# An S4 convolution and a shift mixer in one kernel: two of four inverse groups of the first half moved from the last steps of a loop to behind it

## The chip, the cores and the metric

The kernel runs on one core of a Trainium2 chip. The core has five engines that run side by side, each through its own list of instructions, in order: PE (TensorE, matrix products), DVE (VectorE), ACT (ScalarE), POOL (GpSimd) and SP (SyncE, which here issues most of the DMAs). An instruction that waits for a semaphore holds up everything behind it on its own engine. The metric is the time of one execution on the device in microseconds (us). The kernel before took 711.11 us, the median of three runs between 710.77 and 711.17.

## The reference

One batch of 2048 tokens with 512 channels passes through two blocks, each behind a layer norm that is scaled and shifted by a vector made from a condition `c`, and each added back to the input:

```python
sa, ca, ga, sb, cb, gb = split of silu(c) @ w_mod
h = layernorm(x) * (1 + ca) + sa
x = x + ga * A(h)          # A: convolution over the tokens
h = layernorm(x) * (1 + cb) + sb
x = x + gb * B(h)          # B: token shift mixer, then channel MLP

# A: K[d, l] = Re sum_n C[d, n] * exp(dt*A[d, n]*l) * dt*B[d, n], N = 128
Yf = rfft(pad(u)) * rfft(pad(K));  y = irfft(Yf)[:, :L] + u * Dskip
# B, with D = 512, F = 1376
h = gelu(layernorm(x) @ w1)
g0..g3 = the four quarters of h's channels, shifted by +1, -1, +2, -2 tokens
x1 = x + concat(g0..g3) @ w2
out = x1 + gelu(layernorm(x1) @ w3) @ w4
```

All of it is float32.

## The kernel before

*Matrix products.* The kernel makes its float32 products either directly, or, for the four weights W1 to W4, in three passes: each operand is split into a high part (rounded to the faster type fp32r) and a low part, and high times high, low times high and high times low are summed (`three`, L825, L826, L828). The high part of a split is an ACT copy, the low part a DVE subtraction.

*The convolution* is a Fourier transform cut in stages. First the kernel K and the input are brought into spectra in part; then a loop of 16 steps, `steps = [(jh, kc)]`, goes over two halves of the channels (`jh`, 256 channels each, steps 0 to 7 and 8 to 15) and eight blocks of frequencies (`kc`). A step multiplies the spectrum of K (`spectrum_k`, L667, TensorE) with that of the input (`multiply`, L678, L679 and L683, DVE), takes the previous step's product a stage back (`back`, L693, TensorE, written to a scratch tensor `ZT[jh]` in memory by a POOL DMA), prepares the next step's input spectrum (`spectrum_u`, L644) and loads a block three steps ahead (`load_vu`).

*The inverse groups.* What is left of the inverse transform of a half is done in four groups of four token blocks (there are 16 token blocks of 128 tokens). `load_inv(jh, g)` reloads two blocks of `ZT[jh]`; `inv_half(jh, g, i, ...)` makes eight matmuls (L722) into one PSUM tile and returns a function that, when called, lets DVE add that tile to the resident sequence `X2`, which the trace calls `KX` (L725). `inverse(jh, g)` does both halves `i` of a group, matmuls and addition in turn. The loop makes groups 0, 1 and 2 of the first half in steps 11, 12 and 13, with their loads issued in steps 9 to 12. Group 3 is made behind the loop, and so are all groups of the second half.

*Memory that several stages share.* Loaded blocks lie in a ring of seven buffers (`block`, named `ld`): the VU blocks, the reloaded blocks of `ZT`, and the raw halves of W1 and W2 (`ldw1`, `ldw2` with `two`) on their way to being split. A buffer is used again when its last reader is done. When the convolution is over, the pools that hold the ring are closed (`a2.close()`, `a12.close()`) and the weights W3 and W4 (`pw34`) are laid over their memory; the tile of W4's low part, which is also where W4's raw values are loaded, covers the addresses of the ring.

*The tail.* From the end of the loop on the order is written out by hand. `back` of step 15; the reload of `ZT[1]`; inverse group 3 of the first half; ten `half_stat` (L772), which take the layer norm's statistics over the first 256 channels of one token block each; the second half of W2 is loaded (`split = ldw2(two, 2, 2)`), and its `split()` stands further down; `keep(n)` (L1139), n matmuls whose result is not used; the inverse groups of the second half. Then the mixer runs over eight groups of 256 tokens, in the order 7, 0, 1, 2, 3 here and 4, 5, 6 inside the channel groups: `mix_mod1`, `mix_mod2` (scale and shift, statistics on DVE, the reciprocal root and the negated mean on POOL, L814 and L815), `mix_norm` (ACT), `transposed` (TensorE, L790: eight transposes of a 128x128 tile, each an entry of (channel block k, token block i), into two PSUM tiles, the first for k = 0 and 1, the second for k = 2 and 3), `parts_of` (ACT's copy and DVE's subtraction, L798), `mix_half` (twice 48 matmuls with W1 through `mix_w`, then gelu to a tile `go`, and its store to a scratch tensor `GD` by SP, L837). `load_w(c)` issues a third of W3's and W4's loads on SP (L738). The shift by 1 or 2 tokens is made by reading `GD` at an offset: `chan_load(g)` issues four loads of the windows of a channel group (L860), `chan_split` splits them (the ACT copy `wh`), and `chan_sum` multiplies them with W2 (L879, L880, L882).

*The channel groups.* `chan(0)` to `chan(7)`, 256 tokens each, run W3 (L825, L826, L828) and W4 (L941, L942, L949) with gelu between, and carry along the next group's preparation.

All engines take their work in the order in which the code emits it (`tc.manual_schedule()`): there is no planner, and no due times.

Of the kernel before, what the change touches and what calls it, by code (L numbers as in the profile page):

```python
# [111 lines left out]
def body(ctx, tc, A):  # L112
# [403 lines left out]
    for k in range(8):  # L516
        w, i = ("w3", k) if k < 4 else ("w4", k - 4)
        n = A[w].shape[0] // 4
# [182 lines left out]
    def load_inv(jh, g, i=None, qs=(Y, Y)):  # L701
        if (jh, g) not in zis:
            zis[jh, g] = [block() for h in range(2)]
        for h in range(2):
            c0 = 12 - 4 * g if h == 0 else 4 * g
            a, n = (0, 4) if i is None else (2 * (i if h else 1 - i), 2)
            qs[h].dma_start(zis[jh, g][h][:, a:a + n],
                            dram(ZT[jh], (h * 16 + c0 + a) * 32768, [[256, 128], [32768, n], [1, 256]]))
# [6 lines left out]
    def inv_half(jh, g, i, pl, name):  # L715
        zz = zis[jh, g]
        p = pl.tile([128, 2, 256], F32, name=name)
        for e in range(2):
            for h in range(2):
                b = g * 4 + i * 2 + e  # L720
                cc = 15 - b if h == 0 else b
                T.matmul(p[h * 64:h * 64 + 64, e], FI[:, cc, h], zz[h][:, cc % 4],  # L722
                         start=True, stop=True, skip_group_check=True)
        x = X2[:, g * 4 + i * 2:g * 4 + i * 2 + 2, jh * 256:jh * 256 + 256]
        return lambda: V.tensor_add(x, p, x)  # L725

    def inverse(jh, g):
        for i in range(2):
            inv_half(jh, g, i, psy, "py")()

    def weights(pl, src, rows, cols, name, ntile):
        hi = pl.tile([128, ntile, cols], F32R, name=name + "h")
# [38 lines left out]
    def half_stat(b, jh):  # L771
        V.bn_stats(st1[:, (b + 2) % 16, jh], X2[:, b, jh * 256:jh * 256 + 256])  # L772
# [12 lines left out]

    def transposed(x):
        ps = [psT.tile([128, 2, 256], F32, name=f"pT{j}") for j in range(2)]
        for k in range(4):
            for i in range(2):
                T.transpose(ps[k // 2][:, k % 2, i * 128:i * 128 + 128], x[:, i, k * 128:k * 128 + 128], ident)  # L790
        return ps

# [290 lines left out]
    with tc.manual_schedule():  # L1083
        t3 = A["T3"].rearrange("p (a b) -> p a b", a=32)
        load_vu(*steps[0])
        Y.dma_start(T3[:, :16], t3[:, :16])
        Y.dma_start(Gm, A["G"].rearrange("p (a b) -> p a b", a=2))
        for r in range(8):
            k_first(r)
            if r == 3:  # L1090
                load_vu(*steps[1])
            if r == 6:
                load_vu(*steps[2])
        us = spectrum_u(*steps[0])
        split = None
        for n, st in enumerate(steps):
            p = spectrum_k(*st)
            multiply(*st, us, p)
            if n == 7:
                v0x.close()  # L1100
                pw2 = ctx.enter_context(pool("pw2", side="right", reuse_waits="tile"))
                pw1 = ctx.enter_context(pool("pw1", side="right", reuse_waits="tile"))
                W2h, W2l, ldw2 = weights(pw2, A["w2"], 512, 512, "w2", 4)
                W1h, W1l, ldw1 = weights(pw1, A["w1"], 512, 512, "w1", 4)
            if n > 0:
                back(*steps[n - 1])
            if n < 15:
                us = spectrum_u(*steps[n + 1])
            if n + 3 < 16:
                load_vu(*steps[n + 3])  # L1110
            if n == 0:
                load_t2(1)
            if n == 1:
                Y.dma_start(T3[:, 16:], t3[:, 16:])
            if n in (3, 4, 6, 8):
                load_x(n - 3 if n < 5 else n // 2 - 1)
            if n == 9:
                Y.dma_start(FI, A["FI"].rearrange("p (a b c) -> p a b c", a=16, b=2))
            if split:
                split()  # L1120
                split = None
            if n in (8, 9, 14):
                split = (ldw1 if n < 10 else ldw2)(two, n % 2 * 2, 2)
            if 9 <= n < 13:
                load_inv(0, n - 9)
            if 11 <= n < 14:
                inverse(0, n - 11)
        back(*steps[15])
        s2x.close()
        tp = lambda name, bufs=1, **k: pool(name, bufs, reuse_waits="tile", **k)  # L1130
        cm = ctx.enter_context(tp("cm", 2, side="right"))
        hv = ctx.enter_context(tp("hv", side="right"))
        gop = ctx.enter_context(tp("gop", 2, side="right"))
        psT = ctx.enter_context(tp("psT", space=PSUM))
        psw = ctx.enter_context(tp("psw", 2, space=PSUM))
        def keep(n):
            d = psT.tile([128, 2, 256], F32, name="pT0").rearrange("p a b -> p (a b)")
            for _ in range(n):
                T.matmul(d, W1h[:, 0, :128], W1h[:, 0], start=True, stop=True)  # L1139

        load_inv(1, 3, 1, (Y, S))
        load_inv(1, 0, 0, (Y, S))
        load_inv(1, 3, 0)
        load_inv(1, 0, 1)
        inverse(0, 3)
        for b in (14, 15, 0, 1, 2, 3, 4, 5, 6, 7):
            half_stat(b, 0)
        load_inv(1, 1)
        split = ldw2(two, 2, 2)
        keep(14)  # L1150
        inv_half(1, 3, 1, psy, "py")()
        first_stats(7)
        load_inv(1, 2)
        a00 = inv_half(1, 0, 0, psy, "py")
        a30 = inv_half(1, 3, 0, psw, "pm")
        a01 = inv_half(1, 0, 1, psw, "pm")
        keep(22)
        mix_mod1(7)
        mix_mod2(7, 0)
        mix_mod2(7, 1)  # L1160
        a00()
        mix_norm(7)
        first_stats(0)
        a30()
        a01()
        mix_mod1(0)
        hl = parts_of(transposed(mh.pop(7)[0]))
        mix_mod2(0, 0)
        mix_mod2(0, 1)
        split()  # L1170
        a10 = inv_half(1, 1, 0, psy, "py")
        a11 = inv_half(1, 1, 1, psy, "py")
        mix_half(7, hl, 0)
        mix_norm(0)
        first_stats(1)
        a10()
        mix_half(7, hl, 1)
        mix_mod1(1)
        hl = parts_of(transposed(mh.pop(0)[0]))
        mix_mod2(1, 0)  # L1180
        mix_mod2(1, 1)
        a11()
        mix_half(0, hl, 0)
        a20 = inv_half(1, 2, 0, psy, "py")
        mix_norm(1)
        first_stats(2)
        mix_half(0, hl, 1)
        a21 = inv_half(1, 2, 1, psy, "py")
        mix_mod1(2)
        hl = parts_of(transposed(mh.pop(1)[0]))  # L1190
        mix_mod2(2, 0)
        a20()
        mix_mod2(2, 1)
        a21()
        a2.close()
        a12.close()
        pw34 = ctx.enter_context(tp("pw34"))
        W3h, W3l, ldw3 = weights(pw34, WD["w3"], 512, 1376, "w3", 4)
        W4h, W4l, ldw4 = weights(pw34, WD["w4"], 1376, 512, "w4", 11)
        c2p = ctx.enter_context(tp("c2p", 2))  # L1200
        psm = ctx.enter_context(tp("psm", 2, space=PSUM))
        load_w(0)
        mix_half(1, hl, 0)
        mix_norm(2)
        first_stats(3)
        mix_half(1, hl, 1)
        chan_load(0)
        mix_mod1(3)
        hl = parts_of(transposed(mh.pop(2)[0]))
        mix_mod2(3, 0)  # L1210
        mix_mod2(3, 1)
        load_w(1)
        load_w(2)
        mix_half(2, hl, 0)
        chan_split(0)
        mix_norm(3)
        chan_mod(0, 0)
        mix_half(2, hl, 1)
        add0 = chan_sum(0, 0)
        chan_mod(0, 1)  # L1220
        add0()
        hl = parts_of(transposed(mh.pop(3)[0]))
        add1 = chan_sum(0, 1)
        split_w(1)
        n = cm.tile([128, 2, 512], F32, name="h2")
        sm = [(cm.tile([128, 2], F32, name="cmv"), cm.tile([128, 1], F32, name="crs")) for i in range(2)]

        def stat0(i):
            stats(sm[i][0], cn[0][:, i])
            rstd(sm[i][1], sm[i][0][:, 1:2])  # L1230

        def norm0(i):
            V.tensor_scalar(n[:, i], cn[0][:, i], sm[i][0][:, 0:1], sm[i][1], op0=OP.subtract, op1=OP.mult)

        stat0(0)
        split_w(1)
        add1()
        mix_half(3, hl, 0)
        stat0(1)
        norm0(0)  # L1240
        norm0(1)
        split_w(1)
        mix_half(3, hl, 1)
        r = transposed(n)
        split_w(1)
        r = parts_of(r)
        split_w(4)
        chan_add(0)
        first_stats(4)
        chan_load(1)  # L1250
        for g in range(8):
            r = chan(g, r)
# [18 lines left out]
```

## Time and profile before

| what | us |
|---|---|
| median of three runs | 711.11 |
| the profiled execution | 710.0 |
| its span, first to last instruction | 708.2 |
| TensorE busy | 670.5 (95%) |
| its weight loads | 518.3 (73%) |
| DVE busy | 500.1 (71%) |
| ACT busy | 336.0 (47%) |
| POOL busy | 91.5 (13%) |

A profile shows one execution. "Span" is the time from the first to the last instruction; the execution's own time is a little longer. A matmul's weight load runs beside other matmuls and is listed apart. A row of a timeline gives the start in us, the duration, the engine, the line of the code, the operation with its output and inputs by the program's names, and after x how many instructions of that kind are run together in the row; the bracket at the end says how long the engine had been idle ahead of it and what released it, the releaser being inferred. A row whose engine reads DMA is a transfer, from its issue's completion to its landing. A row whose engine ends in q, as SPq, is the queue of that engine issuing DMAs or waiting to. In a table by stretches each row is one stretch of time, with the busy time of each engine in it and the number of instructions in brackets.

### The profile page before, as it was taken

To read this page: it belongs to the slowest core of one execution; us is meant where nothing else is said; L and a number is where in the kernel's file an instruction comes from. 1 tells how busy PE (TensorE), PEld (TensorE's weight loads), DVE (VectorE), ACT (ScalarE), POOL (GpSimd) and SP (SyncE) were. 2 spreads that over 40 slices of the span, in tenths; PEclk is the share of its full clock that TensorE was granted. 3 is DMA by queue.
4 is the path that set the end of the run, shared out by engine and by line. 5 is a ranking of instruction groups with operands and counts; after the bars stand their busy time and mean duration, and the time that the engine had idled before them with its cause. 6 is when DMAs were issued, how large, how long until landed. Compare 5 with 4: busy or idle time off the path is not lost.

```text
span 708.2 us, 16836 instructions
## 1 busy us (share of the span) xinstructions
PE 670.5 (95%) x7083; PEld 518.3 (73%) x7083; DVE 500.1 (71%) x827; ACT 336.0 (47%) x553; POOL 91.5 (13%) x203
## 2 busy tenths in 40 slices
PE   1899999999999999997999899999999999999997
PEld 0456655666568655654788789899898988989896
DVE  7799999999986765776988868467454536354522
ACT  3878898889956454542444633314132221212120
POOL 4011112021000000000563101001020000000000
PEclk9999999999999999999999999999999999999999
DMA  8903274745349997965559211011110201111011
GB/s 285 285 2 83 65 219 117 199 103 174 84 105 348 252 274 259 300 208 184 189 187 321 65 31 31 16 45 31 39 52 16 60 16 36 25 31 31 0 31 31
DMA packets 56627, 85.51 MB, mean 121 GB/s; under 512 B 5508, under 2 KB 43400, under 8 KB 54888
## 3 DMA queue, kind: packets, MB, share of 16 engines
q1 hardware_dynamic: 52536, 66.87, 33.4%
q0 software_dynamic: 3136, 16.52, 6.7%
q8 instruction: 56, 0.92, 0.6%
q10 hardware_dynamic: 880, 1.05, 0.5%
q14 instruction: 19, 0.16, 0.1%
HBM read 58.20 MB, written 31.85 MB: 127 GB/s over the span
## 4 chain that ended last, share of the span: by engine, by line
PE 46%; DMA 4%; DVE 2%; ACT 1%; SPq 1%; issue 1%; ACTq 0%; DVEq 0%
PE pm L825 7%; PE pm L826 7%; PE pm L828 7%; PE pa L949 6%; PE pa L941 6%; PE pa L942 6%; PE ph L880 2%; PE ph L882 2%; PE ph L879 2%; DMA GD<-go 2%; PE pT L790 2%; DMA ld<-ZT 1%; DMA w4l<-Dw 1%; PE pT L1139 1%; SPq L738 1%
## 5 line engine op out<-in xcount | busy, mean ns | idle before, releaser
L120 ACT ACTIVATE gh<-pm 128x512 fp32r<-128x512 f32 (+1 forms) x48 | 26.9, 561 | 200.6 <-PE pm L828 200.6
L825 PE MATMUL pm<-nh,w3h 128*128 128x256 f32 (+1 forms) x352 | 85.8, 279 | 0.9 <-ACT nh L120 0.9
L826 PE MATMUL pm<-nh,w3l 128*128 128x256 f32 (+1 forms) x352 | 85.7, 279 | 0.1
L933 DVE TENSOR_TENSOR gl<-gf,gh 128x512 fp32r<-128x512 f32 (+1 forms) x48 | 30.8, 642 | 68.4 <-ACT gf L120 68.4
L941 PE MATMUL pa<-w4h,gh 128*128 128x512 f32 (+1 forms) x176 | 69.6, 396 | 0.0
L942 PE MATMUL pa<-w4l,gh 128*128 128x512 f32 (+1 forms) x176 | 68.9, 392 | 0.0
L825 PEld LDWEIGHTS pm<-nh,w3h 128*128 128x128 f32 (+1 forms) x352 | 65.3, 185 | 2.6 <-ACT nh L120 1.1
L826 PEld LDWEIGHTS pm<-nh,w3l 128*128 128x128 f32 (+1 forms) x352 | 65.3, 185 | 2.2 <-DVE w3l L744 0.5
L828 PE MATMUL pm<-nl,w3h 128*128 128x256 f32 (+1 forms) x352 | 54.8, 277 | 0.0
L949 PE MATMUL pa<-w4h,gl 128*128 128x512 f32 (+1 forms) x176 | 48.1, 390 | 0.8 <-DVE gl L933 0.8
L457 PE MATMUL xx<-MG,ON 64*128 64x512 f32 x160 | 48.1, 397 | 0.0
L458 PE MATMUL xx<-MG,ON 64*128 64x512 f32 x160 | 48.0, 396 | 0.0
L753 POOL TENSOR_TENSOR rs<-mv,eps_t 128x1 f32<-128x1 f32 (+1 forms) x39 | 11.9, 306 | 277.8 <-DVE mv L759 265.8
L828 PEld LDWEIGHTS pm<-nl,w3h 128*128 128x128 f32 (+1 forms) x352 | 46.7, 185 | 0.2 <-DVE nl L798 0.2
L885 DVE TENSOR_TENSOR h<-h,ph 128x512 f32<-128x512 f32 x16 | 11.0, 687 | 45.1 <-PE ph L882 45.1
L475 DVE SCALAR_TENSOR_TENSOR e<-tr,p 128x512 f32<-128x512 f32 x64 | 41.0, 682 | 1.5 <-ACT tr L120 1.4
L120 ACT ACTIVATE z<-pz 128x512 f32<-128x512 f32 x32 | 17.4, 595 | 51.9 <-issue 25.1
L678 DVE TENSOR_TENSOR ma<-pk,us 128x512 f32<-128x512 f32 x32 | 21.9, 685 | 27.3 <-issue 16.1
L507 PEld LDWEIGHTS kp<-e,e 128*32 128x32 f32 x2048 | 30.1, 110 | 12.7 <-issue 8.2
L949 PEld LDWEIGHTS pa<-w4h,gl 128*128 128x128 f32 (+1 forms) x176 | 33.0, 188 | 8.3 <-DVE gl L933 1.2
L484 DVE TENSOR_TENSOR e<-tr,p 128x1024 f32<-128x1024 f32 x32 | 38.9, 1216 | 0.0
L485 DVE TENSOR_TENSOR e<-tr,m 128x1024 f32<-128x1024 f32 x32 | 38.9, 1216 | 0.0
(230 smaller groups left out, 1758.3 us busy)
## 6 DMA issues: line engine op xcount, KB each, us to landing
VU<-vs SPq DMA_DIRECT2D x64, 128.0 KB, 3.4
ld<-VU SPq DMA_DIRECT2D x16, 512.0 KB, 14.5
ZT<-z POOLq DMA_DIRECT2D x15, 512.0 KB, 6.3
ld<-ZT SPq DMA_DIRECT2D x12, 512.0 KB, 6.2
Dw<-in_w POOLq DMA_DIRECT2D x8, 688.0 KB, 4.7
xu<-in_u SPq DMA_DIRECT2D x16, 256.0 KB, 8.1
KX<-in_u SPq DMA_DIRECT2D x16, 256.0 KB, 12.6
GD<-go SPq DMA_DIRECT2D x16, 256.0 KB, 2.2
```

The costliest lines, as they stand in the source:

```text
L120: return S.activation(out, in_, f, bias=bias, scale=scale)
L457: T.matmul(x[:, :512], la, ma, start=(i == 0), stop=(i == len(ops) - 1))
L458: T.matmul(x[:, 512:], lb, mb, start=(i == 0), stop=(i == len(ops) - 1))
L475: V.scalar_tensor_tensor(e0[:, 1, a], tr[:, 1, 0], 1.0 - 2.0 * a, mg[:, a], op0=OP.mult, op1=OP.mult)
L484: V.tensor_mul(e0[:, 0], tr[:, 0, 0:1].to_broadcast([128, 2, 512]), mg)
L485: V.tensor_mul(e1.rearrange("p r d q -> p r (d q)"), tr[:, :, 1], m1s[0][:, u % 2:u % 2 + 1].to_broadcast([128, 2, 512]))
L825: T.matmul(p, wh[:, k, c], hi[k], start=(k == 0), stop=False)
L826: T.matmul(p, wl[:, k, c], hi[k], start=False, stop=False)
L828: T.matmul(p, wh[:, k, c], lo[k], start=False, stop=(k == 3))
L941: T.matmul(acc[i], gh[:m, e, s], W4h[:m, f], start=(f == 0), stop=False)
L942: T.matmul(acc[i], gh[:m, e, s], W4l[:m, f], start=False, stop=False)
L949: T.matmul(acc[i], gl[:m, e, s], W4h[:m, f], start=False, stop=(f == 10))
```

## The change

It does five things.

1. Inverse groups 1 and 2 of the first half leave steps 12 and 13. Group 1's 16 matmuls are issued in step 15, behind `back` of step 14, and its two additions behind the loop, ahead of `back` of step 15. Group 2 goes ahead of group 3, behind the loop. Their reloads of `ZT[0]`, and group 3's, move from steps 10, 11 and 12 to steps 13, 13 and 14.
2. Four of the ten `half_stat` (token blocks 0 to 3, which belong to group 0) go into step 12; six stay in the tail.
3. The two fillers get shorter: `keep(14)` becomes `keep(6)`, and `keep(22)` becomes `keep(14)`.
4. The eight transposes of `transposed` are issued by token block, i = 0 with all four k first, then i = 1, where before each k came with both i. It applies to every mixer group and every channel group.
5. The `split()` of W2's second half moves from ahead of the inverse group (1, 1) to behind the last addition of the convolution, `a21()`, just ahead of the closing of the pools.

```diff
+    def inverse_parts(jh, g):
+        return [inv_half(jh, g, i, psy, "py") for i in range(2)]
+
     def inverse(jh, g):
-        for i in range(2):
-            inv_half(jh, g, i, psy, "py")()
+        for f in inverse_parts(jh, g):
+            f()
...
     def transposed(x):
         ps = [psT.tile([128, 2, 256], F32, name=f"pT{j}") for j in range(2)]
-        for k in range(4):
-            for i in range(2):
+        for i in range(2):
+            for k in range(4):
...
             if n > 0:
                 back(*steps[n - 1])
+            if n == 15:
+                i1 = inverse_parts(0, 1)
...
-            if 9 <= n < 13:
-                load_inv(0, n - 9)
-            if 11 <= n < 14:
-                inverse(0, n - 11)
+            if n == 9:
+                load_inv(0, 0)
+            if n == 11:
+                inverse(0, 0)
+            if n == 12:
+                for b in range(4):
+                    half_stat(b, 0)
+            if n == 13:
+                load_inv(0, 1)
+                load_inv(0, 2)
+            if n == 14:
+                load_inv(0, 3)
+        for f in i1:
+            f()
         back(*steps[15])
...
         load_inv(1, 0, 1)
+        inverse(0, 2)
         inverse(0, 3)
-        for b in (14, 15, 0, 1, 2, 3, 4, 5, 6, 7):
+        for b in (14, 15, 4, 5, 6, 7):
             half_stat(b, 0)
         load_inv(1, 1)
         split = ldw2(two, 2, 2)
-        keep(14)
+        keep(6)
         inv_half(1, 3, 1, psy, "py")()
...
-        keep(22)
+        keep(14)
         mix_mod1(7)
...
         mix_mod2(0, 1)
-        split()
         a10 = inv_half(1, 1, 0, psy, "py")
...
         a21()
+        split()
         a2.close()
```

`inverse` now emits the matmuls of both halves ahead of the first addition; the order on TensorE and the order on DVE are each the same by that.

## The prediction

> **What bounds the kernel now.** Three views, in this order: the page's head and chain, the stretches of the steps and of what follows, and the timelines between the last steps and the first channel group.
>
> ```profile
> span 708.2 us, 16836 instructions
> PE 670.5 (95%) x7083; PEld 518.3 (73%) x7083; DVE 500.1 (71%) x827; ACT 336.0 (47%) x553; POOL 91.5 (13%) x203
> PE 46%; DMA 4%; DVE 2%; ACT 1%; SPq 1%; issue 1%; ACTq 0%; DVEq 0%
> ...
> 290.77:298.20 7.43, 7.43 (x106) 4.63 (x104) 6.65 (x14) 4.89 (x14) 0.72 (x2) 1.00 1.04 352
> 298.20:305.63 7.43, 7.43 (x106) 4.63 (x104) 5.21 (x10) 2.80 (x8) 0.53 (x1) 1.00 0.95 289
> 305.63:313.06 7.43, 7.43 (x106) 4.63 (x104) 5.20 (x10) 2.80 (x8) 0.53 (x1) 1.00 0.89 297
> 313.06:318.76 5.70, 5.70 (x90) 3.48 (x88) 4.31 (x9) 1.72 (x5) 0.34 (x1) 1.00 0.07 24
> ...
> 345.01:404.00 58.99, 55.45 (x410) 49.15 (x410) 50.80 (x96) 31.93 (x53) 24.98 (x64) 1.00 0.55 177
> 404.00:708.20 304.20, 298.89 (x1911) 269.33 (x1911) 158.74 (x262) 74.59 (x139) 17.82 (x46) 1.00 0.11 30
> ```
>
> TensorE is the bound. Columns of the stretches: length, then busy time of PE, its weight loads, DVE, ACT and POOL, granted clock, DMA share, GB/s. The first four are steps 11 to 14, cut at the first L667 matmul of each: TensorE is busy for all of a step, and a step with an inverse group is 1.73 us longer (7.43 against 5.70). From 404 us on TensorE works 298.89 of 304.20 us with the other engines well below, so whatever moves the start of that stretch moves the end of the kernel one for one. The change touches only what lies between 298 and 404 us, where TensorE does wait:
>
> ```profile
> 320.67 1.99 PE L693 MATMUL pz<-zc,Gm 64*128 64x512 f32 x8
> 324.48 1.99 PE L693 MATMUL pz<-zc,Gm 64*128 64x512 f32 x8 [1.82 <-ACT w2h L120]
> 326.39 1.95 PE L722 MATMUL py<-ld,FI 128*64 128x256 f32 x16
> 328.27 3.47 PE L1139 MATMUL pT<-w1h 128*128 128x512 f32 x14
> 333.54 3.09 PE L722 MATMUL py<-ld,FI 128*64 128x256 f32 x16 [1.80 <-DMA ld<-ZT]
> 339.57 5.28 PE L1139 MATMUL pT<-w1h 128*128 128x512 f32 x22
> 345.01 1.06 PE L790 MATMUL pT<-ident,h 128*128 128x128 f32 x8
> 346.00 1.95 PE L722 MATMUL py<-ld,FI 128*64 128x256 f32 x16
> 372.10 0.98 PE L790 MATMUL pT<-ident,h 128*128 128x128 f32 x7 [1.08 <-ACT h L120]
> ```
>
> There is a hole of 1.82 us between the last two `back` calls, filler (`keep`, L1139) of 3.47 and 5.28 us around the reload of ZT, and a wait for a normalised tile. The hole's releaser is misnamed: `back(15)` needs DVE's third `zc`, which ends at 324.33 (row below).
>
> **The change, part by part.** I keep the clock of the old trace and subtract the loop's gain at the end.
>
> *The loop.* Steps 12 and 13 lose an inverse group each: 2 x (7.43 - 5.70) = 3.46 us. Does another engine take over? Step 12 gets four half statistics, at 0.337 us each (3.37 / 10, below) 1.35 us, behind DVE's multiply (3.74 us, by the starts of its rows); 5.1 us fit in 5.70. The loads move later in SP's order, but a VU load then no longer stands behind two loads of ZT, and the loads of groups 1 to 3 wait only for ring blocks that steps 10 to 14 free; the last, freed by step 14, are needed some 13 us later. At 5.70 us each, steps 12 and 13 are like step 14. If this cover is gone, both ends are 0 and 3.46; I take 3.46.
>
> *Group 1 and group 2.* Group 1's 16 matmuls (1.95 us in the row) go into the hole of 1.82 us: 0, at most 0.1 us. Its two additions follow W2's split on DVE:
>
> ```profile
> 323.92 0.41 DVE L683 TENSOR_TENSOR zc<-ma 128x256 f32<-128x256 f32 x1
> 324.59 1.28 DVE L744 TENSOR_TENSOR w2l<-ld,w2h 128x512 fp32r<-128x512 f32 x2
> 329.14 3.37 DVE L772 BATCH_NORM_STATS2 st<-KX 128x6 f32<-128x256 f32 x10
> 335.18 0.69 DVE L725 TENSOR_TENSOR KX<-py,KX 128x512 f32<-128x512 f32 x1 [2.67 <-PE py L722]
> 346.30 1.29 DVE L798 TENSOR_TENSOR nl<-pT,nh 128x512 fp32r<-128x512 f32 x2 [0.44 <-ACT nh L120]
> 350.69 1.28 DVE L744 TENSOR_TENSOR w2l<-ld,w2h 128x512 fp32r<-128x512 f32 x2
> 369.79 0.66 DVE L725 TENSOR_TENSOR KX<-py,KX 128x512 f32<-128x512 f32 x1
> ```
>
> Groups 2 and 3 then alternate with the additions over two PSUM buffers: 16 matmuls more (1.9 us) and additions of 0.69, so the last half of group 3 ends on TensorE near 330.8, its addition near 331.5, six half statistics (2.0 us) near 333.5, and `keep(6)` (0.24 us each) near 332.2. All of it lies before 333.54, when the reload lands, and before DVE's next work at 335.18: 0. The reload itself,
>
> ```profile
> 327.63 2.24 DMA ZT<-z
> 332.46 6.06 DMA ld<-ZT
> ```
>
> hangs on `back(15)`, not on the groups. Its blocks of (1, 0) and (1, 1) now come free with groups 2 and 3, near 328.9 and 330.8, while their issues stand at 330.4 and 333.5: 0, with 1.5 us to spare.
>
> *keep(14) for keep(22).* The filler ends at 339.57 + 14 x 0.24 = 342.9. Then the normalised tiles bind:
>
> ```profile
> 341.77 0.82 ACT L120 ACTIVATE h<-h,nm,rs 128x512 f32<-128x512 f32 x1 [14.17 <-POOL nm L815]
> 342.97 0.82 ACT L120 ACTIVATE h<-h,nm,rs 128x512 f32<-128x512 f32 x1 [0.38 <-POOL nm L815]
> ```
>
> *Transposes by block.* The first block's four run at 342.9, the second's from 343.85 to 344.4: the pair's end comes 1.65 us before 346.07. Elsewhere the new order has two signs: the first PSUM half is full after six transposes instead of four (0.24 us late where TensorE binds), and only four are left behind a late second block (0.4 us early, as at 372.10). I take 0 for the rest.
>
> What of the 1.65 us lives on? DVE loses its wait of 0.44 at 346.30, and the W2 split (1.28) leaves its place at 350.69; but mod2, statistics and POOL's square root of the next group stand before that split, so the next transposes gain only 0.44 to 0.8. I take 0.8 for everything up to SP's weight loads.
>
> *The moved split.* This is the price. W4's tile lies over the ring's blocks, so its first load waits until every block under it is free, the one with W2's second half included, that is until the moved split's two DVE subtractions are done. Behind it on SP stand, in order:
>
> ```profile
> 365.49 1.86 SPq L738 DMA_DIRECT2D w3l<-Dw  x4
> 367.45 1.80 SPq L738 DMA_DIRECT2D w4l<-Dw  x4
> 369.35 3.58 SPq L837 DMA_DIRECT2D GD<-go  x2
> 372.98 3.34 SPq L860 DMA_DIRECT2D win<-GD  x4
> 376.38 1.85 SPq L738 DMA_DIRECT2D w3l<-Dw  x4
> ...
> 385.15 7.65 SPq L837 DMA_DIRECT2D GD<-go  x4
> ...
> 369.35 5.63 DMA GD<-go
> ...
> 378.21 1.06 ACT L120 ACTIVATE wh<-win 128x1024 fp32r<-128x1024 f32 x1 [0.94 <-DMA win<-GD]
> 390.76 0.60 ACT L120 ACTIVATE go<-pm 128x512 f32<-128x512 f32 x1 [5.79 <-DMA GD<-go]
> ...
> GD<-go SPq DMA_DIRECT2D x16, 256.0 KB, 2.2
> ```
>
> The split now follows a21's addition, which ends at 370.45; less 0.8, less the 1.28 that left DVE before it, that is 368.4, and 1.28 more makes 369.7 to 370.1: W4's loads start 2.5 us late. The store of go(1, 0) goes out at 371.9 instead of 369.35. Before, it landed at 374.98, behind eight loads; now four of these are long done. Ends: 2.2 us after its issue (median in the last row), 374.1, and 5.63, 377.5. With four loads still ahead I take 376.2, 1.2 us late. The window loads wait for it, ACT's `wh` for them, `chan_sum` on TensorE for that; the other weights and stores follow on SP, and gelu at 390.76 waits for such a store's buffer. So the first channel group starts 1.2 us late on this clock.
>
> [...]
>
> **Sum.** -3.46 + 0 + 1.2 = -2.3 us (the 0.8 is in the 1.2). The profiled execution took 710.0 us (span 708.2), so 707.7; the median of the runs is 711.11, 1.1 above it, so 708.8.
>
> **Rivals.**
> *The store lands 2.2 us after its issue*, as most do: 374.1 is even earlier than 374.98, SP's delay costs nothing, and up to 0.8 of the tail's gain survives: -3.5 to -4.3, 706.8 to 707.6. For it: the four w3l loads are over by then; against: four 256 KB loads stand in the same queue. 0.20.
> *The whole delay passes.* W4's loads start 2.5 to 3.1 us late (3.1 without the 0.8) and nothing behind them is absorbed: -0.4 to -1.0, 710.1 to 710.7. Against: SP stood waiting for go(1, 1) until some 372.6 anyway (the row 369.35 + 3.58 ends with that second issue). 0.12.
> *Slower: W4's wait decides.* If DVE gains nothing, the split ends at 370.45 + 1.28 = 371.7, 4.3 late; if the store then again lands 7.53 us after W4's first issue, 379.2, 4.2 late; if the reads of windows and the remaining weights collide with it and the gelu at 390.76 loses the longest excess seen (5.63 - 2.2 = 3.4) once more in part, the tail loses 5 to 7. From 4.9 on (3.46 + 1.4) the kernel is slower: 712.6 to 714. For it: these stores stand in the chain at 369.35 and hold up gelu at 390.76. 0.17.
> *The steps do not shorten*, because a load or DVE binds them: 0 + 1.2, 712.3; against: step 14 is such a step. 0.05.
> *TensorE's clock drops.* With `chan_sum` 1.2 us late and mix_half(2, 1) early, TensorE idles some 2.4 us near 380. If its matmuls then took twice as long over `chan_sum`, twelve of the filler's size (0.24 each), that is +2.9: 711.7. [...] 0.04.
>
> **How the numbers follow.** The forecast has 0.42, with its own range 707.9 to 709.6 (store between its ends). What a measurement can tell from no change is 0.2%, 1.4 us: faster means under 709.7, slower over 712.5. Faster: 0.42 + 0.20 = 0.62. Same: whole delay 0.12, clock 0.04, and 0.03 of the steps' 0.05: 0.19. Slower: W4's wait 0.17 and the steps' other 0.02: 0.19. The range for 8 in 10 reaches from 706.6 (all of the tail's gain) to 712.4.
>
> **What would show it.** Steps 12 and 13 at 5.70; L722 matmuls in front of the last L693; the first L790 row in two parts, near 339.5 and 340.4; SP's first w4l some 5 us after its first w3l, with the split's L744 just before; L825 on W3 starting near 391.2 instead of 393.47. Wrong if the w4l loads do not wait (then 707), or if L860's loads come more than 3 us later against w3l than they do now.

## The result: no change in time, and the loop's gain taken back behind a wait of SyncE

The changed kernel took 711.38 us (median of 20 runs), the kernel before 710.78 us in as many; the ratio is 1.0006, with a 95% interval of 0.9991 to 1.0020. That is inside the range and within what a measurement tells from no change. The forecast of 708.8 us, 2.3 us under before, did not come.

The page's head of the changed kernel:

```profile
span 709.2 us, 16806 instructions
PE 668.3 (94%) x7067; PEld 515.9 (73%) x7067; DVE 500.4 (71%) x827; ACT 337.1 (48%) x553; POOL 91.5 (13%) x203
```

Two executions can only be compared from a common point, because the code ahead of step 11, in which the kernels differ by no more than one reload, ends at another time in each: step 11 begins at 290.77 us in the profile before and at 291.48 after. I therefore measure from the first spectrum matmul of step 11 to the first W3 matmul: **102.70 us before** (393.47 less 290.77) and **103.09 us after** (394.57 less 291.48). What follows is 314.7 and 314.6. So in the profiles the changed part is 0.4 us longer. The stretches of the changed kernel (columns as in the prediction): steps 11 to 14, then from the first transposes to the first W3 matmul, then the rest.

```profile
291.48:298.91 7.43, 7.43 (x107) 4.63 (x105) 6.65 (x14) 4.89 (x14) 0.71 (x2) 1.00 1.06 360
298.91:304.61 5.70, 5.70 (x90) 3.48 (x89) 4.31 (x9) 1.73 (x5) 0.35 (x1) 1.00 1.01 318
304.61:310.31 5.70, 5.70 (x90) 3.48 (x88) 5.14 (x13) 2.79 (x9) 0.53 (x2) 1.00 0.64 189
310.31:316.01 5.70, 5.70 (x90) 3.48 (x88) 3.82 (x9) 2.79 (x9) 0.53 (x2) 1.00 0.64 188
340.61:394.57 53.96, 47.40 (x344) 41.86 (x344) 42.09 (x79) 23.70 (x39) 23.57 (x63) 0.97 0.58 190
394.57:709.20 314.63, 308.53 (x1976) 277.75 (x1976) 169.22 (x281) 84.04 (x155) 19.97 (x50) 1.00 0.12 32
```

Steps 12 and 13 are 5.70 us, as forecast. But in the fifth row the granted clock is 0.97, in a stretch where it was 1.00 before. TensorE's timeline up to the first transposes:

```profile
317.92 1.99 PE L693 MATMUL pz<-zc,Gm 64*128 64x512 f32 x8
319.84 1.95 PE L722 MATMUL py<-ld,FI 128*64 128x256 f32 x16
321.73 1.99 PE L693 MATMUL pz<-zc,Gm 64*128 64x512 f32 x8
323.78 3.85 PE L722 MATMUL py<-ld,FI 128*64 128x256 f32 x32
327.56 1.65 PE L1154 MATMUL pT<-w1h 128*128 128x512 f32 x6
330.72 3.03 PE L722 MATMUL py<-ld,FI 128*64 128x256 f32 x16 [1.50 <-DMA ld<-ZT]
...
336.99 3.47 PE L1154 MATMUL pT<-w1h 128*128 128x512 f32 x14
340.61 1.06 PE L793 MATMUL pT<-ident,h 128*128 128x128 f32 x8
```

Group 1 fills the hole between the two `back` calls, groups 2 and 3 and six fillers lie ahead of the reload. The first transposes stand 49.13 us behind step 11's start (340.61 less 291.48) against 54.24 before (345.01 less 290.77): 5.11 us gained, the loop's 3.46 and the 1.65 of the shorter filler. All of it is lost again within the next 45 us. VectorE's split of W2's second half, SyncE's queue, ScalarE's copy of the windows, and TensorE around the W2 product, all of the changed kernel:

```profile
366.16 1.29 DVE L747 TENSOR_TENSOR w2l<-ld,w2h 128x512 fp32r<-128x512 f32 x2
...
361.24 1.86 SPq L741 DMA_DIRECT2D w3l<-Dw  x4
367.47 1.74 SPq L741 DMA_DIRECT2D w4l<-Dw  x4
369.32 0.89 SPq L840 DMA_DIRECT2D GD<-go  x2
370.26 5.02 SPq L863 DMA_DIRECT2D win<-GD  x4
...
369.32 4.61 DMA GD<-go
373.99 0.33 SPq L863
...
377.70 1.06 ACT L120 ACTIVATE wh<-win 128x1024 fp32r<-128x1024 f32 x1 [3.06 <-DMA win<-GD]
...
378.81 0.50 PE L882 MATMUL ph<-w2h,wh 128*128 128x512 f32 x1 [2.94 <-ACT wh L120]
380.23 0.63 PE L882 MATMUL ph<-w2h,wh 128*128 128x512 f32 x1
383.26 1.03 PE L793 MATMUL pT<-ident,h 128*128 128x128 f32 x8
```

W4's first load goes out at 367.47, 0.02 us after the split's end (366.16 + 1.29), and 4.4 us after W3's fourth load was issued (361.24 + 1.86). The store behind it starts at 369.32 and lands 4.61 us later, at 373.93; the second window load, which waits for it, goes out at 373.99, the last of the four is issued at 375.28 (370.26 + 5.02), and TensorE stands still for 2.94 us ahead of the W2 product. Then that product runs slowly: a matmul takes 0.63 us. In the kernel before it took 0.39, and the second window load went out here:

```profile
375.04 0.33 SPq L860
...
380.36 0.39 PE L879 MATMUL ph<-w2h,wh 128*128 128x512 f32 x1
...
382.21 1.04 PE L790 MATMUL pT<-ident,h 128*128 128x128 f32 x8
```

The stretches of 2 us of the changed kernel say why; the third number from the end is the granted clock:

```profile
376.00:378.00 2.00, 0.00 (x0) 0.00 (x0) 0.00 (x0) 0.30 (x1) 0.00 (x0) 1.00 0.96 243
378.00:380.00 2.00, 1.19 (x4) 1.01 (x5) 1.21 (x2) 2.00 (x3) 0.00 (x0) 0.84 0.99 338
380.00:382.00 2.00, 2.00 (x7) 1.54 (x6) 1.96 (x4) 0.65 (x2) 0.00 (x0) 0.50 1.00 347
382.00:384.00 2.00, 2.00 (x12) 1.68 (x11) 1.42 (x3) 0.00 (x0) 0.00 (x0) 0.81 1.09 405
384.00:386.00 2.00, 2.00 (x12) 1.65 (x11) 1.40 (x4) 1.89 (x4) 0.00 (x0) 1.00 1.03 376
```

Behind the gap the clock is halved, to 0.50. From the W2 product's start to the transposes behind its first part it takes 4.45 us (378.81 to 383.26) instead of 2.89 (379.32 in the kernel before, to 382.21): 1.56 us. It is no peculiarity of this execution: the median of the mean clock over a whole execution is 0.992 in 20 of the changed kernel, and 0.996 in 35 of the kernel before that were taken with the experiments.

### The profile page after: what moved, and what is told of

Read it like the earlier page. It is cut to its first block, busy times and chain, and to the rows that moved or that the text cites. A ratio compares the mean times of both kernels' runs of the same rounds, so it can differ in the third digit from the quotient of the medians.

```text
span 709.2 us, 16806 instructions
## 1 busy us (share of the span) xinstructions
PE 668.3 (94%) x7067; PEld 515.9 (73%) x7067; DVE 500.4 (71%) x827; ACT 337.1 (48%) x553; POOL 91.5 (13%) x203
## 4 chain that ended last, share of the span: by engine, by line
PE 77%; DVE 15%; ACT 3%; issue 2%; DMA 2%; SPq 0%; POOL 0%; DVEq 0%; ACTq 0%
PE pm L828 7%; PE pm L829 7%; PE pm L831 7%; PE pa L952 6%; PE pa L944 6%; PE pa L945 6%; PE xx L457 5%; PE pk L667 4%; PE pk L644 4%; PE pz L693 4%; PE kp L507 3%; PE ph L882 2%; PE ph L883 2%; PE ph L885 2%; DVE e L475 2%
## 5 line engine op out<-in xcount | busy, mean ns | idle before, releaser
L457 PE MATMUL xx<-MG,ON 64*128 64x512 f32 x160 | 47.1, 390 | 0.0
L458 PE MATMUL xx<-MG,ON 64*128 64x512 f32 x160 | 47.1, 390 | 0.0
```

The costliest lines, as they stand in the source:

```text
L457: T.matmul(x[:, :512], la, ma, start=(i == 0), stop=(i == len(ops) - 1))
L458: T.matmul(x[:, 512:], lb, mb, start=(i == 0), stop=(i == len(ops) - 1))
```

## The experiments

All were timed against the kernel before. The stretch is the one defined above, from one profile each; the ratio comes from some 8 to 12 runs.

| kernel | step 11 | first W3 matmul | stretch | ratio (95%) |
|---|---|---|---|---|
| before | 290.77 | 393.47 | 102.70 | |
| changed | 291.48 | 394.57 | 103.09 | 1.0006 (0.9991 to 1.0020) |
| split_back | 290.94 | 390.46 | 99.52 | 0.9959 (0.9937 to 0.9982) |
| split_only | 291.97 | 400.48 | 108.51 | 1.0045 (1.0018 to 1.0071) |
| fill_gap | 288.35 | 390.48 | 102.13 | 0.9997 (0.9972 to 1.0022) |
| w4_later | 289.50 | 390.30 | 100.80 | 0.9966 (0.9948 to 0.9985) |
| loop_only | 289.70 | 389.45 | 99.75 | 0.9950 (0.9928 to 0.9971) |
| tr_only | 290.37 | 393.95 | 103.58 | 0.9994 (0.9972 to 1.0016) |
| loads_later | 290.56 | 390.50 | 99.94 | 0.9938 (0.9914 to 0.9963) |
| loads_later_back | 291.95 | 391.92 | 99.97 | 0.9952 (0.9926 to 0.9979) |
| fill_both | 289.97 | 391.95 | 101.98 | 1.0010 (0.9993 to 1.0027) |
| loads_later_fill | 287.97 | 387.35 | 99.38 | 0.9942 (0.9920 to 0.9964) |
| no_fill | 294.38 | 396.68 | 102.30 | 1.0004 (0.9979 to 1.0030) |

**The split back at its old place.** On the changed kernel:

```diff
         mix_mod2(0, 1)
+        split()
         a10 = inv_half(1, 1, 0, psy, "py")
...
         a21()
-        split()
         a2.close()
```

> The changed kernel with only the split of W2's second half put back ahead of the inverse group (1, 1). Measure: the stretch from the first spectrum matmul of step 11 to the first W3 matmul, 102.70 us before (290.77 to 393.47) and 103.09 after (291.48 to 394.57); what follows is 314.7 in both. Theory (the moved split lets W4's loads wait, these hold up the store and the window loads behind them on SyncE): W4's first load follows W3's fourth within 1 us, no gap of 2.94 us ahead of the W2 product, no half clock there, stretch 98.6 to 99.4, time 3.5 to 4.3 us under before (ratio about 0.994 to 0.995). Rival 1 (the order of the steps only hands its time to another wait of the tail, whatever stands on SyncE): stretch 102 to 103, ratio 0.999 to 1.001. Rival 2 (the split at its old place delays the mixer's groups on VectorE by its 1.28 us, and this is what it was moved for): stretch 100 to 100.7.

Measured: 99.52 us and 0.9959. VectorE's split, SyncE's W4 loads, the W2 product and the first W3 matmul:

```profile
347.05 1.27 DVE L747 TENSOR_TENSOR w2l<-ld,w2h 128x512 fp32r<-128x512 f32 x2
...
363.78 1.81 SPq L741 DMA_DIRECT2D w4l<-Dw  x4
...
376.23 0.51 PE L882 MATMUL ph<-w2h,wh 128*128 128x512 f32 x1 [0.46 <-ACT wh L120]
...
390.46 0.39 PE L828 MATMUL pm<-nh,w3h 128*128 128x256 f32 x1 [0.87 <-ACT nh L120]
```

W4's loads follow W3's at once (the fourth of these was issued at 363.69), the gap is 0.46 us, the clock stays at 1.00 here. The theory holds, 0.1 us outside its stretch and with a ratio a little nearer to 1 than expected; both rivals fall. One line moved back is worth 3.6 us of the stretch.

**The moved split alone**, on the kernel before:

```diff
         mix_mod2(0, 1)
-        split()
...
         a21()
+        split()
         a2.close()
```

> The kernel before with only the split of W2's second half moved behind the last addition of the convolution. Theory (W4's wait): the split ends near 371.3 on the clock of before, W4's first load goes out some 4 us late, the store behind it at about 373.2 and lands 4.7 us later, the windows' copy wh starts near 381.6 instead of 378.2, TensorE waits about 3.4 us ahead of the W2 product and then runs it at half clock (1.6 us more): stretch 107 to 108 instead of 102.70, time 4 to 5 us over before (ratio about 1.006 to 1.007). Rival 1 (no cost in the split's place): 102.7, ratio 1.000. Rival 2 (VectorE gains the 1.28 us): 101.5 to 102.3, ratio under 1.

Measured: 108.51 us and 1.0045. VectorE, SyncE, TensorE, and one stretch of 2 us:

```profile
371.46 1.28 DVE L744 TENSOR_TENSOR w2l<-ld,w2h 128x512 fp32r<-128x512 f32 x2
...
366.51 1.88 SPq L738 DMA_DIRECT2D w3l<-Dw  x4
372.78 1.74 SPq L738 DMA_DIRECT2D w4l<-Dw  x4
...
384.76 0.50 PE L879 MATMUL ph<-w2h,wh 128*128 128x512 f32 x1 [2.32 <-ACT wh L120]
...
386.00:388.00 2.00, 2.00 (x6) 1.52 (x6) 1.97 (x3) 0.60 (x2) 0.00 (x0) 0.50 1.01 358
```

Again W4's first load stands right behind the split's end (371.46 + 1.28 = 372.74), and again the clock is 0.50 behind the gap, which here is 2.32 us. The wait and the fall come with this one move, in either kernel. The stretch is 0.5 us over the expected one; in this execution the clock fell once more, near 376. The ratio, expected at 1.006 to 1.007, is 1.0045; its interval gives 1.3 to 5.0 us.

**W4's first loads behind the windows**, on the changed kernel, the split left where the change put it:

```diff
+    def load_w3(c):
+        for i in range(4):
+            splits.append(ldw3(None, i, 1, 0, 512))
+    def load_w4(c):
+        for f in range(4):
+            splits.append(ldw4(None, f))
...
-        load_w(0)
+        load_w3(0)
...
         chan_load(0)
+        load_w4(0)
```

> The changed kernel with the first four loads of W4 issued behind the four window loads of the first channel group instead of ahead of the store of the mixer's group 1; the split stays where the change put it. Theory (W4's wait costs only what stands behind it on SyncE): the store goes out near 364.7 and 368.9, the windows land by 374, wh near 374.5, no gap ahead of the W2 product and no half clock, stretch 98.6 to 99.5, ratio 0.994 to 0.995, as with the split back at its place. Rival 1 (the windows wait for the stores to land whatever is queued, 4.7 us each): wh stays near 377, stretch 102 to 103. Rival 2 (W4's loads, later, are missed by the W4 split of the first channel group): the wait shows there, stretch good but what follows is longer than 314.7.

Measured: 0.9966, where 0.994 to 0.995 was expected (the interval begins at 0.9948), and 100.80 us, which is 1.3 more than the range. The windows' side came as expected: no gap ahead of the W2 product, at full clock. But ScalarE's gelu of group 3 and TensorE's first W3 matmul:

```profile
387.64 0.60 ACT L120 ACTIVATE go<-pm 128x512 f32<-128x512 f32 x1 [7.86 <-DMA GD<-go]
...
390.30 0.39 PE L828 MATMUL pm<-nh,w3h 128*128 128x256 f32 x1 [3.10 <-ACT nh L120]
```

The next bound is a store of group 2, which stands behind all loads of W3 and W4, and behind the gap of 3.10 us the clock fell once more, to 0.50 between 392 and 394 us. So the late split itself costs nothing up to the W2 product, which starts 84.42 us behind step 11 here and 85.29 in split_back; what stands behind W4's load on SyncE makes its price.

**Filler in the gap**, on the changed kernel:

```diff
+        keep(11)
         add0 = chan_sum(0, 0)
```

> The changed kernel with eleven filler matmuls of 0.24 us (a second product of W1 that nothing uses) ahead of the W2 product, in the gap of 2.94 us there. Theory (the gap itself brings the clock down to 0.50, and the 24 matmuls of the W2 product behind it pay for it): the W2 product starts where it did, 378.81 less 291.48 = 87.3 us behind step 11, its first part takes 2.9 us to the transposes instead of 4.45, granted clock 1.00, stretch 101.5, time 1.6 us under the changed kernel (ratio to before about 0.998). Rival (the clock falls for another cause, such as the DMA traffic of that time, which stands at 0.96 to 1.09 of its engines): the clock falls all the same, stretch 103.

Measured: 102.13 us and 0.9997, where 101.5 and about 0.998 were expected. The W2 product kept its clock, and from its start to the transposes took 2.80 us. But the clock fell elsewhere in this execution, after 1.23 us of idle time in the midst of the transposes of group 2:

```profile
366.00:368.00 2.00, 1.53 (x10) 1.45 (x10) 2.00 (x5) 0.99 (x2) 1.20 (x2) 0.85 0.98 302
368.00:370.00 2.00, 2.00 (x10) 2.00 (x10) 1.93 (x5) 0.00 (x0) 0.25 (x1) 0.50 0.91 294
```

**Filler there too**:

```diff
+        keep(4)
         hl = parts_of(transposed(mh.pop(2)[0]))
...
+        keep(11)
         add0 = chan_sum(0, 0)
```

> The kernel fill_gap with four filler matmuls more, ahead of the transposes of the mixer's group 2. In fill_gap the W2 product kept its clock, but in that execution the clock fell to 0.50 earlier, behind the wait of 1.23 us for that group's second normalised block (363.60 to 367.4, four transposes and 1.7 us of idle time). Theory (the clock falls after idle time wherever it is, for some 3.4 us, and costs about 1.6 us each time): no stretch of 2 us between 318 and 404 us shows a clock under 0.99, stretch from step 11 to the first W3 matmul 101.2 to 101.9 instead of 103.09 in the changed kernel, ratio 0.997 to 0.999. Rival (the clock falls for another cause, such as the traffic of W3 and W4 at that time): it falls again between 366 and 384, stretch 102.5 to 104.

Measured: no fall anywhere between 318 and 404 us, and 101.98 us, 0.1 over the expected range. The W2 product's first matmul and a stretch of 2 us:

```profile
377.44 0.50 PE L882 MATMUL ph<-w2h,wh 128*128 128x512 f32 x1 [0.28 <-ACT wh L120]
...
378.00:380.00 2.00, 2.00 (x10) 1.63 (x9) 1.97 (x3) 1.28 (x3) 0.00 (x0) 1.00 0.99 348
```

So in this place it was the idle time that brought the clock down and not the traffic, whose share is 0.99 here as it was in the changed kernel. Over whole executions, too, the median of the mean clock rises from 0.992 to 0.9945. The times don't confirm the price: 1.0010, where 0.997 to 0.999 was expected. The profile's 1.1 us (103.09 less 101.98) lies within the intervals of both kernels; that the fall costs this place 1.1 to 1.6 us is read from single profiles, and what it costs of the whole time stays open.

**The loop's part alone**, on the kernel before: the groups, their loads and the four half statistics as in the change, without the fillers, the transposes and the split.

```diff
-            if 9 <= n < 13:
-                load_inv(0, n - 9)
-            if 11 <= n < 14:
-                inverse(0, n - 11)
...
+        for f in i1:
+            f()
...
+        inverse(0, 2)
         inverse(0, 3)
-        for b in (14, 15, 0, 1, 2, 3, 4, 5, 6, 7):
+        for b in (14, 15, 4, 5, 6, 7):
```

> The kernel before with only the groups, their loads and the four half statistics moved as in the change; fillers of 14 and 22, the old order of the transposes and the split at its old place. Same measure as before (step 11's first spectrum matmul to the first W3 matmul: 102.70 before, 103.09 in the changed kernel, 99.52 with the split back). Theory (the loop's 3.46 us are the whole gain, fillers and transposes add nothing that reaches the end): 99.2 to 99.6, ratio 0.994 to 0.997, as with the split back. Rival (the shorter fillers and the new transposes carry part of the gain of the kernel with the split back): 100.5 to 101.5, ratio about 0.998.

Measured: 99.75 us, 0.15 over the theory's range and far from the rival's, and 0.9950; that is 2.95 us off the stretch. Step 12 and the first transposes:

```profile
297.13:302.83 5.70, 5.70 (x90) 3.48 (x88) 4.31 (x9) 1.73 (x5) 0.35 (x1) 1.00 1.02 317
...
340.81 1.06 PE L793 MATMUL pT<-ident,h 128*128 128x128 f32 x8
```

The transposes come 3.13 us earlier than before (51.11 against 54.24), not 5.11 as in the changed kernel; at the first W3 matmul there are only 0.23 us between this kernel and split_back (99.52). Fillers and transposes move their own place and not the end.

**The fillers taken away**, on loop_only:

```diff
-        keep(14)
...
-        keep(22)
```

> The kernel loop_only without its two rows of filler (14 and 22). TensorE then idles some 3.5 us ahead of the reload's matmuls and some 3.3 to 4.3 us ahead of the first transposes. Theory (idle time brings the clock down, and the fillers are there against it): a clock of 0.50 shows behind one or both gaps, between 329 and 346 us; the transposes come up to 1.2 us earlier, but the half clock costs 1.6 us in the mixer's group 7: stretch 100.2 to 102 instead of 99.75, ratio 0.996 to 0.999. Rival 1 (the fillers only take TensorE's time): stretch 98.5 to 99.7, no fall of the clock. Rival 2 (the clock falls, but the wait for the windows' landing hides it): clock 0.50 and stretch 99.5 to 100.

Measured: 102.30 us, 0.3 over the theory's range, and 1.0004, a little over it. The gaps, and two of the stretches of 2 us behind them:

```profile
333.99 3.27 PE L722 MATMUL py<-ld,FI 128*64 128x256 f32 x15 [3.46 <-DMA ld<-ZT]
...
343.93 0.47 PE L793 MATMUL pT<-ident,h 128*128 128x128 f32 x1 [3.86 <-ACT h L120]
...
346.00:348.00 2.00, 2.00 (x11) 1.26 (x11) 2.00 (x4) 1.68 (x4) 0.00 (x0) 0.50 0.00 0
348.00:350.00 2.00, 2.00 (x12) 0.95 (x8) 1.93 (x5) 1.84 (x3) 0.00 (x0) 0.50 0.00 0
```

The clock falls at the end of both gaps (0.81 between 332 and 334 us, 0.87 between 342 and 344) and stays low behind them, in these two rows with no DMA traffic in the last column. Without its useless matmuls the kernel is 2.55 us longer in the stretch and 0.54% in the ratios (1.0004 against 0.9950): here the clock's price shows in the times too, though the 5.14 us that the clock takes here between 318 and 404 us (2 us times what it lacks to 1.00) are three times the 1.70 of the changed kernel.

**The transposes alone**, on the kernel before:

```diff
-        for k in range(4):
-            for i in range(2):
+        for i in range(2):
+            for k in range(4):
```

> The kernel before with only the transposes issued by token block. The prediction took 0 for this part: stretch 102.3 to 103.1, what follows 314.7, ratio 0.999 to 1.001. Rival 1 (where a normalised tile comes late, only four transposes are left behind it, 0.4 us at the pair at 372.10): stretch 102.2 or less. Rival 2 (the first PSUM half is full two transposes later in all sixteen groups, 0.24 us each in the channel groups): what follows is 316 to 318, ratio 1.002 to 1.005.

Measured: 0.9994 and 103.58 us; what follows took 314.6, so rival 2 falls. The stretch is 0.5 us over the range. At group 2 the second block's four transposes stand behind a wait of 0.75 us, where seven stood behind 1.08 before:

```profile
372.13 0.66 PE L790 MATMUL pT<-ident,h 128*128 128x128 f32 x4 [0.75 <-ACT h L120]
```

The W2 product then waits 0.35 us for the windows; whether the order of the transposes has a part in the 0.9 us, or only the landing of the stores, one profile does not tell. The times say that it is nothing or at most 0.3% to either side.

**Later loads**, on w4_later (loads_later), and with the split at its old place (loads_later_back):

```diff
         load_w(1)
-        load_w(2)
...
         chan_load(1)
+        load_w(2)
```

> The kernel w4_later with the last third of the loads of W3 and W4 (seven, 1.4 MB) issued behind the windows of the second channel group too, so that the stores of the mixer's group 2 no longer stand behind them. In w4_later the first part of the W2 product was over 4.1 us earlier than before, but gelu of group 3 waited 7.86 us for such a store, TensorE 3.10 us ahead of the first W3 matmul, and the clock fell to 0.50 behind it. Theory (that store's place in the queue was the next bound): gelu's wait under 5 us, gap ahead of W3 about 0.9 as before, stretch 98.3 to 99.0 instead of 100.80, what follows 314.7, ratio 0.994 to 0.995. Rival (the eight loads of the second third alone hold the store up as long): stretch 100 to 101.

> The same two moves of loads with the split of W2's second half at its old place. Theory (once no wait stands ahead of SyncE's queue, the split's place is worth at most the 0.4 to 0.8 us that VectorE loses ahead of the mixer's group 0): stretch 98.3 to 99.8. Rival (W4's wait still counts somewhere when the split is behind): stretch shorter than that of loads_later by over 1 us.

Measured: 99.94 us and 0.9938; 99.97 us and 0.9952, so both stretches lie over their ranges, by 0.9 and 0.2 us. TensorE's two waits in loads_later:

```profile
367.97 0.66 PE L793 MATMUL pT<-ident,h 128*128 128x128 f32 x4 [1.24 <-ACT h L120]
...
390.50 0.39 PE L828 MATMUL pm<-nh,w3h 128*128 128x256 f32 x1 [0.87 <-ACT nh L120]
```

The gap ahead of W3 is back at 0.87, so the store's place was w4_later's bound. The rest of the expected gain is missing. In loads_later the clock fell near 370 behind the gap of 1.24 us, to 0.50 between 370 and 372; but loads_later_back, where it did not fall between 318 and 404 us, is no shorter, and its W2 product waits 1.09 us for the windows. So the fall alone does not explain the missing time. With no wait ahead of SyncE's queue, the split's place makes no difference (0.03 us of stretch). The same four fillers as above were put into loads_later:

> The kernel loads_later with the same four filler matmuls ahead of the transposes of group 2. In loads_later's execution the clock fell to 0.50 near 370 behind a gap of 1.24 us, and the stretch was 99.93. Theory: no fall, stretch 98.3 to 98.9, ratio 0.992 to 0.994. Rival (the windows' landing bounds this place, the clock only takes what would be waited for anyway): stretch 99.5 to 100.2 and a gap ahead of the W2 product of over 0.5 us.

Measured: no fall, 99.38 us and 0.9942. That is 0.5 us more than the theory's range, without the gap that the rival named; so these profiles give the fall 0.6 us of stretch; the ratio is that of loads_later. Its median, 705.99 us against 710.57 of the kernel before in the same series, is the lowest of all. The six kernels in which nothing urgent stands behind W4's wait lie between 0.9938 and 0.9966, and their intervals overlap: all are faster than the two kernels of the case, by 0.3 to 0.6%, and which of them is best stays open.

## Why the prediction was right or wrong

*The loop:* right. -3.46 us in the rows of steps 12 and 13, with VectorE at 5.14 us in the stretch that holds the four half statistics (forecast 5.1). Alone it is worth 2.95 us of stretch and 0.50% of the time.

*Groups 1 and 2, at 0:* right. Group 1 lies in the former hole, the reload's matmuls start 39.24 us behind step 11 (330.72 less 291.48) instead of 42.77, which is the loop's gain to within 0.1 us.

*keep(14) for keep(22):* right at its place, 1.65 us. That some of it lives on up to SyncE's weight loads was right as well; I had put 0.8 and it was 1.5: W3's first load stands 69.76 us behind step 11 against 74.72, 4.96 less, of which the loop has 3.46. It took two parts of the change together: with the split back W3's first load stands at 70.89, and 0.4 is left; with nothing but the split moved (split_only) it stands at 74.54, 0.2 less than before. It reached the end in none of the kernels: with the split back, 0.23 us is left of it, since the window loads bind there.

*Transposes, at 0:* not contradicted by the times. The sign that I named did not come: the first eight transposes ran in one row, at 340.61, and not in two parts.

*The moved split:* the mechanism was right, the size was not. On the clock of before, the loop's gain left out, W4's loads were to start 2.5 us late and started 2.8 late (75.99 us behind step 11 against 76.68, and 3.46 to add). The store was to cost 1.2 us. The second window load, which waits for it, was issued at 375.04 before and at 373.99 after, 1.7 us late in the same reckoning; `wh` at 378.21 and 377.70, which is 2.24 us late. So the term of 1.2 was mis-sized: the store landed half a microsecond later than I took, and the windows half a microsecond more behind it. The rival "the whole delay passes" (2.5 to 3.1 us) was nearer to this wait than the forecast was. Two of my signs stood at their limit: W4's first load went out 6.2 us behind W3's first, where I had said some 5, and against W3's first load the first window load came 1.5 us later than before and the second 3.2 us, where more than 3 was to count against the forecast.

*The clock:* this is the step that failed. I gave its fall a chance of 0.04, as a rival beside the forecast, with a price of 2.9 us. It was not another case but the consequence of the forecast's own wait: TensorE idle ahead of the W2 product, forecast 2.4 us, measured 2.94. The price was 1.56, because the slow time, from 379.35 to 382.8 us, ends before the product's first part does (378.81 to 383.26). The sum is then -3.46 + 2.24 + 1.56 = +0.34, against +0.39 measured in the stretch of these two profiles.

I had given it so little because no row that I had taken of before showed a fall and the longest gap shown was 1.82 us. That was an argument from gaps that this kernel fills: no_fill shows what the two rows of filler are for, with 0.50 behind gaps of 3.46 and 3.86 us. It was also an argument from the rows taken: outside them, from 77.4 to 80.6 us, the clock of the profile of before stands at 0.50 too. That the matmuls would take twice as long was an assumption that no row taken of before showed; in the changed kernel one took 0.63 us instead of 0.39. The fall came behind 2.94, 3.46 and 3.86 us, and also behind 2.32 in split_only and behind 1.23 and 1.24 amid short transposes in fill_gap and loads_later. The last section sets the gaps with a fall beside those without.

That rival, with 711.7, also came nearest to the measured 711.38, by luck: its wait was too small (1.2 for 2.24) and its price too large (2.9 for 1.56), and the two errors cancel.

## What to carry to other kernels

A load into memory that another tile still holds waits at the head of its queue, and everything behind it on that queue waits too (here W4's load stood 4.4 us, and a store and four window loads with it): before a buffer's last reader is moved later, look which DMA reuses its memory and what is queued behind that DMA. Moving the load behind the urgent transfers takes the cost away as well as moving the reader back. The five gaps of TensorE of 2.32 to 3.86 us told of here were each followed by a fall of the clock that took 1.7 us of full speed, once 3.4: count such a gap as its length plus up to that, and take filler matmuls out only where no such gap opens.

## What the runs showed of the hardware

*A fall of the clock lasts 3.4 us here, once twice that.* Adding up 2 us times what the clock lacks to 1.00 gives the time at half clock: for the changed kernel 2 x (0.16 + 0.50 + 0.19) = 1.70 us lost, so 3.4 us at 0.50. The falls in the other profiled executions between 318 and 404 us give 1.70 to 1.72 as well, and the second one of no_fill, with 3.42, twice that.

*The length of a gap alone does not tell whether a fall follows.* Idle times of TensorE over 1 us that are told of above or that a timeline shows between 318 and 404 us, in us:

| a fall to 0.50 followed | none followed |
|---|---|
| 1.23 (fill_gap), 1.24 (loads_later), 1.56 and 2.32 (split_only), 2.94 (changed), 3.10 (w4_later), 3.46 and 3.86 (no_fill) | 1.08, 1.80 and 1.82 (before), 1.25 and 1.50 (changed), 1.09 (loads_later_back) |

Waits of 1.23 and 1.25 us at the same place, group 2's second normalised block, brought a fall in fill_gap and none in the changed kernel. Earlier in the execution, too: in the changed kernel the clock also stands at 0.50 from 31.2 to 34.6 us, behind an idle time of 2.29 us, and in the kernel before from 77.4 to 80.6, for 1.71 us lost, where the row ahead of it shows 0.34 us of idle time. So the idle time just ahead is not all that counts; what else does was not shown.

*The part ahead of the change varies most.* Step 11 began between 287.97 and 294.38 us in the thirteen profiles. A change of 1 us in the tail is seen in a stretch of a profile long before the times of whole executions show it; but one profile has one pattern of falls.
